# Transposes of the identity in TensorE's planned gaps, in the first ten pairs of an attention and gated-FFN kernel

## The chip, the cores and the metric

The kernel runs on one core of a Trainium2 chip. The metric is the device time of one execution in microseconds (us): the median of three runs before the change was 793.36 us (792.95 to 796.02).

## The reference

Inputs are q, k and v of shape 8 x 8 x 576 x 64 (batch, heads, sequence, head size), and the weights of a gated FFN. Cut to what matters:

```python
q_rot, k_rot = rotate(q), rotate(k)                      # rotary embedding
scores = (q_rot @ k_rot.T) / sqrt(64)
attn = exp(scores - max(scores)); attn /= sum(attn)      # over the last axis
x = (attn @ v), heads put side by side                   # 8 x 576 x 512
gate = sigmoid(sum over k of conv_w[k] * x shifted by 4 - k)   # 5 taps, causal
out = (gate * (x @ w_val)) @ w_out
```

Weights arrive as 64-bit floats and are decoded on the chip.

## The kernel before

**Work.** Two heads of one batch make a pair; there are 32 pairs, four to a batch. For one pair:

- q and k are loaded, rotated (`rope_mul`, `rope_add`) and split into a high and a low part (`qk_hi`, `qk_lo`).
- `s_mm` computes scores in five chunks, c = 0 to 4, of 128 query rows each: for c = 0 to 3 both heads, 12 matmuls, and for c = 4 the last 64 rows of both heads in 6. Each head's scores go into one PSUM tile `ps_s` of 128 x 2 x 512, two banks, of which columns 0 to 287 of each half are used. There are two such tiles at a time.
- `s_max` (VectorE, DVE) takes the negated row maximum `nm` from `ps_s`; `s_exp` (ScalarE, ACT) reads `ps_s` again and writes the exponentials `p`.
- `t_mm` transposes `p` on TensorE (PE), four blocks of 128 x 128 to a bank `ps_t`; `t_copy` copies them to `pt` in SBUF on ACT or DVE.
- `pv_mm` multiplies `pt` with v (`ps_a`), `x_norm` divides by the row sums, then come five taps (`tap`, most on DVE) and the gate.

After every fourth pair the FFN of that batch follows (`f_mm`, tiles `ps_f`). While the first pairs run, DVE, ACT and GpSimd (POOL) also decode the two weight matrices (`weight_step`, tile `wst`), in 12 pieces.

**Order.** All work is entered as jobs in a `Plan`, each with an engine, a duration in ns and what it reads and writes. `Plan.order` plays the jobs through in a timeline of its own, by these costs and a table of due times; it yields one order for all engines and leaves each job's start and end in `start` and `end`. `Plan.run` then calls the jobs' functions in that order. Each engine works through its instructions strictly in this order. Waits between engines are put in by the framework from the tiles' reads and writes: an instruction that writes a tile waits until those that came earlier in the order and read it have ended. In the plan a transpose costs 108.5 ns.

In the rows of order below, `ident` is the identity, `k_86` and `k_87` the rotated k of even and odd pairs, `q_88` and `q_89` the same for q. A wait on `Activation_49`, `DVE_49`, `Pool_49` or `PE_49` is one for ACT, DVE, POOL or PE itself to have got to a certain instruction. By the diff, line 291 before is line 311 after (`s_mm`), and 316 before is 336 after (`transpose`).

Of the kernel before, what the change touches and what calls it, by code (L numbers as in the profile page):

```python
# [10 lines left out]
F32 = mybir.dt.float32  # L11
# [43 lines left out]
class Plan:  # L55
# [11 lines left out]
    LAG = {"PE": 200, "V": 130, "A": 135, "G": 90, "SP": 100}  # L67
    WAIT = {"PE": 100, "V": 100, "A": 100, "G": 130, "SP": 40}
    SWITCH = 170

    def __init__(self):
        self.jobs = []
# [34 lines left out]
    def order(self, due=None):  # L107
# [40 lines left out]
        while len(done) < n:  # L148
# [11 lines left out]
            if m and m != mode:  # L160
                ns += self.SWITCH
                mode = m
# [17 lines left out]
        self.start, self.end = start, end  # L180
        return done

    def run(self):
        for i in self.order():
            self.jobs[i][3](*self.jobs[i][4])


@with_exitstack
def attn_gated_ffn(ctx: ExitStack, tc: tile.TileContext, q2, k2, v2, tab, w_val, conv_w, w_out, out, collect=None):
# [14 lines left out]
    V, A, G, T, SP = nc.vector, nc.scalar, nc.gpsimd, nc.tensor, nc.sync  # L204
# [9 lines left out]
    psS = ctx.enter_context(tc.tile_pool(name="psS", bufs=B["ps_s"], space=PSUM))  # L214
    psT = ctx.enter_context(tc.tile_pool(name="psT", bufs=B["ps_t"], space=PSUM))

    ident = const.tile([128, 128], F32, name="ident")
# [54 lines left out]
    def qk_lo(p, n, eng, a=0, b=W):  # L272
        t = state[p][n][:, :, a:b]
        eng.tensor_tensor(out=t[:, 1], in0=ins[n][:, 0, a:b], in1=t[:, 0].bitcast(F32), op=ALU.subtract)  # L274

    def s_mm(p, c):


        st = state[p]
        heads = (0,) if c == 4 else (0, 1)  # L280
        tiles = []
        for h in heads:
            ps = psS.tile([128, 2, 512], F32, name="ps_s", tag="ps_s")
            st[f"s{2 * c + h}"] = ps[:, :, 0:288]
            tiles.append(ps)
        for half in range(2):
            for i, (x, y) in enumerate(((0, 0), (0, 1), (1, 0))):
                for h in heads:
                    rows = slice(0, 128) if c == 4 else HEAD[h]
                    k0 = (0 if h else D) + half * 288  # L290
                    T.matmul(out=tiles[h][:, half, 0:288], lhsT=st["q"][rows, x, c * 128:c * 128 + 128],  # L291
                             rhs=st["k"][rows, y, k0:k0 + 288], start=(i == 0), stop=(i == 2))
# [260 lines left out]
    plan = Plan()  # L553
# [38 lines left out]
    for p in range(NP):  # L592
        t = 9 * p
# [31 lines left out]
        for c in range(5):  # L625
            r = kr + " " + toks(f"q{par}#@.@", ("hi", "lo"), (0,) if c < 2 else (1,))
            w = toks(f"ps_s/{p}.@", (2 * c, 2 * c + 1)) if c < 4 else f"ps_s/{p}.8"
            at(f"s{c}", t + 2 * c, "PE", 800, s_mm, p, c, r=r, w=w, mode="r" if c < 4 else "f")
            for i in (2 * c, 2 * c + 1)[:1 + (c < 4)]:
                h = i % 2  # L630
                at(f"max{i}", t + i, "V", 727, s_max, p, i, r=f"ps_s/{p}.{i}", w=f"nm/{p}.{i}")
                at(f"exp{i}", t + i, "A", 830, s_exp, p, i, r=f"ps_s/{p}.{i} nm/{p}.{i}",
                   w=f"p/{p}.{c}#{h} sums{par}#{i}" if i < 8 else f"p/{p}.m sums{par}#8")
# [23 lines left out]
        for g in R2:  # L657
            n = G1 if g else G0
# [58 lines left out]
    if collect is not None:  # L717
        return plan
    with tc.manual_schedule():
        plan.run()  # L720


# [36 lines left out]
def _program(arrays, batches):  # L759
    import concourse.bacc as _bacc  # L760

    nc = _bacc.Bacc("TRN2", target_bir_lowering=False, num_devices=1)
    args = [
        nc.dram_tensor(f"in_{n}", a.shape, mybir.dt.from_np(a.dtype), kind="ExternalInput").ap()
        for n, a in arrays.items()
    ]
    args.append(nc.dram_tensor("out_t", (batches, DM, S), F32, kind="ExternalOutput").ap())
    with tile.TileContext(nc, schedule_with_timeline_sim=True) as tc:
        attn_gated_ffn(tc, *args)
    return nc  # L770
# [9 lines left out]
```

## Time and profile before

| | |
|---|---|
| Median of three runs | 793.36 us |
| The profiled execution, and its span | 798.84 us, 797.0 us |
| PE busy | 730.3 us, 92% |
| PE weight loads (PEld) busy | 589.7 us, 74% |
| DVE busy | 604.5 us, 76% |
| ACT busy | 489.7 us, 61% |
| POOL busy | 414.5 us, 52% |
| Transposes of `p` (L316) | 1312, busy 202.2 us |
| Score matmuls (L291) | 1728, busy 184.4 us |
| Exponentials (L310) | 288, busy 212.0 us |
| Maxima (L297) | 288, busy 209.0 us |

The busy share is a mean over the span. PEclk is the TensorE clock that the throttle granted as a share of full speed; it is 1.00, 0.50 or, over a longer stretch, a mean of the two. In the profile's rows, what stands in brackets is the idle time of the engine ahead of the instruction, and what ended it.

### The profile page before, as it was taken

Reading aid. Unit: us, or ns where it says so; the run is one execution under the profiler, and the core shown is the slowest. Engines: PE = TensorE matmul, PEld = TensorE weight load, DVE = VectorE, ACT = ScalarE, POOL = GpSimd, SP = SyncE. Lnnn points to the kernel's source line nnn. Section 1 sums busy time; section 2 is a strip of 40 time slices with the busy share of each in tenths; the row PEclk is TensorE's granted clock in tenths of the full one; section 3 lists DMA queues with packets and bytes.
Section 4 is the critical chain, followed back from the end, with each engine's and each line's share of the span. In section 5 each row is a group of like instructions: output and inputs, shape, how many; then the busy total and the mean of one; then the engine's idle time right before and its main releaser. Section 6 shows DMA issues by size and latency. Waiting matters only on the chain.

```text
span 797.0 us, 16072 instructions
## 1 busy us (share of the span) xinstructions
PE 730.3 (92%) x5889; PEld 589.7 (74%) x5889; DVE 604.5 (76%) x994; ACT 489.7 (61%) x1155; POOL 414.5 (52%) x300
## 2 busy tenths in 40 slices
PE   1787678769999999999999999999999999999998
PEld 0655455557688878787878788788778887888798
DVE  4777998889987786778778777878677877776650
ACT  1546536654676666767667676766676676766542
POOL 2446454344745765566644665566755664551121
PEclk9989777899999999999999999999999999999999
DMA  7634323223333334433344223333443333410111
GB/s 186 154 83 109 92 74 105 74 57 105 87 93 100 85 77 114 114 104 91 104 109 112 71 71 110 103 90 92 113 115 93 92 101 105 111 37 24 37 47 60
DMA packets 92881, 73.76 MB, mean 93 GB/s; under 512 B 60633, under 2 KB 71426, under 8 KB 92802
## 3 DMA queue, kind: packets, MB, share of 16 engines
q1 hardware_dynamic: 91250, 71.51, 33.7%
q10 hardware_dynamic: 1552, 1.21, 0.6%
q8 instruction: 47, 0.77, 0.4%
q14 instruction: 32, 0.26, 0.1%
HBM read 63.10 MB, written 9.59 MB: 91 GB/s over the span
## 4 chain that ended last, share of the span: by engine, by line
PE 67%; DVE 10%; ACT 2%; issue 2%; DMA 1%; SPq 0%; POOLq 0%; POOL 0%; ACTq 0%; DVEq 0%
PE ps_f L458 22%; PE ps_a L371 16%; PE ps_t L316 15%; PE ps_s L291 15%; DVE nm L297 3%; DVE g L435 2%; ACT p L310 1%; DVE y L466 1%; DVE sums L382 1%; DVE wst L507 1%; DMA kin<-in_k 1%; ACT pt L357 1%; DVE pt L359 1%; PE ps_r L387 0%; DVE kin L263 0%
## 5 line engine op out<-in xcount | busy, mean ns | idle before, releaser
L310 ACT ACTIVATE p<-ps_s,nm 128x576 f32<-128x576 f32 x288 | 212.0, 740 | 120.9 <-DVE nm L297 119.2
L297 DVE TENSOR_REDUCE nm<-ps_s 128x1 f32<-128x576 f32 x288 | 209.0, 750 | 64.9 <-PE ps_s L291 63.0
L316 PE MATMUL ps_t<-ident,p 128*128 128x128 f32 x1312 | 202.2, 290 | 32.8 <-ACT p L310 27.6
L291 PE MATMUL ps_s<-k,q 64*128 64x288 f32 (+1 forms) x1728 | 184.4, 324 | 24.9 <-ACT k L270 16.5
L316 PEld LDWEIGHTS ps_t<-ident,p 128*128 128x128 f32 x1312 | 154.7, 147 | 70.8 <-ACT p L310 35.8
L291 PEld LDWEIGHTS ps_s<-k,q 64*128 64x128 f32 (+1 forms) x1728 | 144.7, 198 | 56.9 <-issue 20.0
L371 PE MATMUL ps_a<-pt,v 128*64 128x320 f32 (+1 forms) x1280 | 174.3, 418 | 0.0
L263 POOL TENSOR_TENSOR qin<-qin,tab_q 128x640 f32<-128x640 f32 x62 | 100.2, 1628 | 99.9 <-DMA qin<-in_q 99.9
L357 ACT COPY pt<-ps_t 128x512 f32<-128x512 f32 (+2 forms) x261 | 119.2, 467 | 35.6 <-PE ps_t L316 33.0
L371 PEld LDWEIGHTS ps_a<-pt,v 128*64 128x64 f32 x1280 | 87.4, 139 | 63.0 <-issue 13.6
L435 DVE SCALAR_TENSOR_TENSOR g<-x,cw,g 128x576 f32<-128x576 f32 (+2 forms) x132 | 117.1, 891 | 2.0 <-ACT g L432 1.8
L458 PE MATMUL ps_f<-y,wout_hi 128*128 128x288 f32 (+2 forms) x512 | 111.2, 304 | 2.4 <-ACT pt L357 2.3
L359 DVE COPY pt<-ps_t 128x512 f32<-128x512 f32 (+1 forms) x155 | 97.1, 629 | 14.3 <-PE ps_t L316 14.1
L274 POOL TENSOR_TENSOR q<-qin,q 128x640 fp32r<-128x640 f32 (+1 forms) x32 | 52.8, 1650 | 74.7 <-ACT q L270 67.9
L458 PEld LDWEIGHTS ps_f<-y,wout_hi 128*128 128x128 f32 x512 | 82.5, 188 | 5.0 <-ACT pt L357 3.5
L422 POOL TENSOR_TENSOR xl<-x,xh 128x576 fp32r<-128x576 f32 (+2 forms) x33 | 45.5, 1379 | 75.2 <-ACT xh L418 71.2
L473 POOL TENSOR_TENSOR y<-y,y 128x288 fp32r<-128x288 f32 (+2 forms) x64 | 55.6, 869 | 53.4 <-ACT y L470 53.3
L458 PE MATMUL ps_f<-xh,wval_hi 128*128 128x288 f32 (+2 forms) x256 | 77.6, 303 | 0.1
L458 PE MATMUL ps_f<-xl,wval_hi 128*128 128x288 f32 (+2 forms) x256 | 77.2, 301 | 0.0
L458 PE MATMUL ps_f<-y,wout_lo 128*128 128x288 f32 (+2 forms) x256 | 77.1, 301 | 0.0
L458 PE MATMUL ps_f<-xh,wval_lo 128*128 128x288 f32 (+2 forms) x256 | 76.0, 297 | 0.0
L267 POOL TENSOR_TENSOR kin<-kin 128x640 f32<-128x640 f32 (+1 forms) x32 | 49.1, 1533 | 34.5 <-DVE kin L263 33.6
(72 smaller groups left out, 784.7 us busy)
## 6 DMA issues: line engine op xcount, KB each, us to landing
kin<-in_k SPq DMA_DIRECT2D x62, 288.0 KB, 3.8
qin<-in_q SPq DMA_DIRECT2D x31, 512.0 KB, 4.2
out_t<-o SPq DMA_DIRECT2D x56, 144.0 KB, 2.9
rb<-rd SPq DMA_DIRECT2D x31, 144.0 KB, 3.0
v<-in_v SPq DMA_DIRECT2D x32, 128.0 KB, 2.3
v<-in_v SPq DMA_DIRECT2D x64, 64.0 KB, 2.3
rb<-rd SPq DMA_DIRECT2D x31, 128.0 KB, 2.9
qin<-in_q SPq DMA_DIRECT2D x64, 32.0 KB, 3.1
```

The costliest lines, as they stand in the source:

```text
L263: eng.tensor_tensor(out=t[:, i, a:b], in0=t[:, i, a:b], in1=tabs[n][:, i, a:b], op=ALU.mult)
L274: eng.tensor_tensor(out=t[:, 1], in0=ins[n][:, 0, a:b], in1=t[:, 0].bitcast(F32), op=ALU.subtract)
L291: T.matmul(out=tiles[h][:, half, 0:288], lhsT=st["q"][rows, x, c * 128:c * 128 + 128], rhs=st["k"][rows, y, k0:k0 + 288], start=(i == 0), ...
L297: V.tensor_reduce(out=st[f"nm{i}"], in_=st[f"s{i}"], axis=AX.XY, op=ALU.max, negate=True)
L310: A.activation(out=pd.rearrange("p (b x) -> p b x", b=2), in_=st[f"s{i}"], func=AF.Exp, bias=st[f"nm{i}"], scale=1.0, accum_out=sums[p % 2 ...
L316: T.transpose(out=bank[0:rows, j * 128:(j + 1) * 128], in_=src, identity=ident)
L357: A.copy(out=dst, in_=src)
L359: V.tensor_copy(out=dst, in_=src)
L371: T.matmul(out=acc[HEAD[h], 0:n], lhsT=st["v"][:, j, h, :], rhs=st[f"pt{g}"][:, at_:at_ + n], start=(j == 0), stop=(j == 4))
L435: V.scalar_tensor_tensor(out=g, in0=x_sb[:, a + k:b + k], scalar=w, in1=g, op0=ALU.mult, op1=ALU.add)
L458: T.matmul(out=acc[:, 0:n], lhsT=wt[w][:, kc, ds], rhs=mv, start=(kc == 0 and i == 0), stop=(kc == NCH - 1 and i == 2))
L473: G.tensor_tensor(out=ffn[b][1][:, dc, lo:hi], in0=ffn[b, "y", dc, lo], in1=ffn[b][0][:, dc, lo:hi].bitcast(F32), op=ALU.subtract)
```

## The change

`Plan.run` now looks, ahead of each PE job, at the plan's own timeline: t is the end of the PE job before (3000 ns at the start), and if the gap from t to the job's start, less 300 ns, holds more than two transposes of 110 ns, and t is under 230000 ns, that many transposes of the identity are issued ahead of the job. They write columns 384 to 511 of the newest `ps_s` tile, which no other instruction reads or writes. The first 80 come ahead of the first scores, and take the tile that these will use (`spare["next"]`).

```diff
+    FILL = (3000, 230000, 300, 110)
...
-    def run(self):
+    def run(self, fill):
+
+        t = self.FILL[0]
         for i in self.order():
+            if self.jobs[i][1] == "PE":
+                n = int((self.start[i] - t - self.FILL[2]) / self.FILL[3])
+                if n > 2 and t < self.FILL[1]:
+                    fill(n)
+                t = self.end[i]
             self.jobs[i][3](*self.jobs[i][4])
...
+    spare = {}
+
+    def fill(n):
+
+        if not spare:
+            spare["now"] = spare["next"] = psS.tile([128, 2, 512], F32, name="ps_s", tag="ps_s")
+        for _ in range(n):
+            T.transpose(out=spare["now"][:, 0, 384:512], in_=ident, identity=ident)
+
...
-            ps = psS.tile([128, 2, 512], F32, name="ps_s", tag="ps_s")
+            ps = spare.pop("next", None)
+            if ps is None:
+                ps = psS.tile([128, 2, 512], F32, name="ps_s", tag="ps_s")
+            spare["now"] = ps
...
-        plan.run()
+        plan.run(fill)
```

There are 374 such transposes: 80 at the start and 294 in 29 bursts of 3 to 21. Without them the order of every engine is the one before. One exponential gains a wait for PE.

PE's first instructions before, from the first scores of pair 0 on:

```order
L291 MATMUL ps_s<-k_86,q_88 128x288 [waits Activation_49]
L291 MATMUL ps_s<-k_86,q_88 128x288
L291 MATMUL ps_s<-k_86,q_88 128x288 [waits DVE_49]
L291 MATMUL ps_s<-k_86,q_88 128x288 x9
L316 MATMUL ps_t<-ident,p 128x128 [waits Activation_49,Pool_49]
L316 MATMUL ps_t<-ident,p 128x128 x3
L291 MATMUL ps_s<-k_86,q_88 128x288 [waits PE_49]
```

and the same place on PE after:

```order
L291 MATMUL ps_s<-ident 128x128 [waits Pool_49]
L291 MATMUL ps_s<-ident 128x128 x79
L311 MATMUL ps_s<-k_86,q_88 128x288 [waits Activation_49]
L311 MATMUL ps_s<-k_86,q_88 128x288
L311 MATMUL ps_s<-k_86,q_88 128x288 [waits DVE_49]
L311 MATMUL ps_s<-k_86,q_88 128x288 x9
L291 MATMUL ps_s<-ident 128x128 [waits Activation_49]
L291 MATMUL ps_s<-ident 128x128 x14
L336 MATMUL ps_t<-ident,p 128x128 x4
```

The first 80 wait only for POOL, which makes the identity. The burst of 15 stands between the scores and the transposes of `p`, and the wait for ACT stands at the burst; the transposes behind it have none of their own.

PE at the end of pair 0 and the start of pair 1 before (41.95 to 45.49 us in the profile):

```order
L316 MATMUL ps_t<-ident,p 128x128 [waits PE_49,Activation_49]
L316 MATMUL ps_t<-ident,p 128x128 [waits PE_49]
L316 MATMUL ps_t<-ident,p 128x128 x3
L291 MATMUL ps_s<-k_87,q_89 128x288
L291 MATMUL ps_s<-k_87,q_89 128x288 [waits PE_49]
L291 MATMUL ps_s<-k_87,q_89 128x288 [waits DVE_49]
L291 MATMUL ps_s<-k_87,q_89 128x288
L291 MATMUL ps_s<-k_87,q_89 128x288 [waits Pool_49]
L291 MATMUL ps_s<-k_87,q_89 128x288 x7
L316 MATMUL ps_t<-ident,p 128x128 [waits Activation_49]
L316 MATMUL ps_t<-ident,p 128x128 x3
```

and the same place on PE after:

```order
L291 MATMUL ps_s<-ident 128x128 [waits Activation_49]
L291 MATMUL ps_s<-ident 128x128 x13
L336 MATMUL ps_t<-ident,p 128x128 [waits PE_49] x2
L336 MATMUL ps_t<-ident,p 128x128 x3
L311 MATMUL ps_s<-k_87,q_89 128x288
L311 MATMUL ps_s<-k_87,q_89 128x288 [waits PE_49]
L311 MATMUL ps_s<-k_87,q_89 128x288 [waits DVE_49]
L311 MATMUL ps_s<-k_87,q_89 128x288
L311 MATMUL ps_s<-k_87,q_89 128x288 [waits Pool_49]
L311 MATMUL ps_s<-k_87,q_89 128x288 x7
L291 MATMUL ps_s<-ident 128x128 [waits Activation_49]
L291 MATMUL ps_s<-ident 128x128 x14
```

Bursts of 14 and 15 now stand ahead of the transposes on both sides of the scores of pair 1, and take over the wait for ACT.

## The prediction

> **What bounds the kernel now.** I read the slices of the page first, then the busy time by stage. Slices are 19.9 us wide.
>
> ```profile
> PE   1787678769999999999999999999999999999998
> DVE  4777998889987786778778777878677877776650
> PEclk9989777899999999999999999999999999999999
> ```
>
> ```profile
> 16.50:39.90 23.40, 17.98 (x87) 13.98 (x88) 18.38 (x32) 11.01 (x25) 10.74 (x9) 1.00 0.62 152
> 39.90:183.30 143.40, 106.81 (x727) 75.96 (x725) 123.05 (x197) 80.31 (x185) 66.41 (x43) 0.81 0.32 87
> 183.30:797.00 613.70, 605.54 (x5079) 499.75 (x5077) 456.62 (x741) 395.68 (x940) 333.22 (x239) 1.00 0.33 89
> ```
>
> Columns: width, then PE, PEld, DVE, ACT and POOL busy, granted clock, DMA. From 183.30 on PE is busy 605.54 of 613.70 us at full clock: it is the bound, and whatever PE is late by at 183.30 is late at the end. Before that PE is busy 106.81 of 143.40 us, DVE 123.05: neither is full. So only this part, where the clock is 0.81 on average, can gain, and a delay there goes to the end.
>
> Next the clock, in stretches of 3.41 us, the length of which all its recorded intervals are multiples. Columns: width, PE busy, clock.
>
> ```profile
> 39.89:43.30 3.41, 1.94 (x20) 1.00 0.23 40
> 43.30:46.71 3.41, 1.63 (x19) 1.00 0.40 136
> 46.71:50.13 3.42, 2.77 (x18) 0.50 0.01 1
> 50.13:53.54 3.41, 3.41 (x20) 0.50 0.29 89
> 60.37:63.78 3.41, 1.07 (x10) 1.00 0.52 127
> 63.78:67.19 3.41, 3.20 (x14) 0.50 0.50 156
> 67.19:70.61 3.42, 2.26 (x22) 1.00 0.00 1
> 84.26:87.67 3.41, 3.41 (x21) 0.50 0.38 141
> 176.42:179.83 3.41, 1.75 (x20) 1.00 0.00 0
> 179.83:183.25 3.42, 3.42 (x21) 0.50 0.60 174
> sum 34.13, PE 24.85; mean PE 2.48
> ```
>
> A stretch with 1.63, 1.07 or 1.75 us of PE work is followed by half clock, one with 1.94 is not: the fall comes somewhere between 1.75 and 1.94 of 3.41 us. From half clock it rises after a nearly full stretch (3.41, 3.20), not after 2.77. So PE work of any kind could hold the clock, if it lies in the idle time.
>
> What half clock costs a group, and where PE idles:
>
> ```profile
> 45.49 0.66 PE L316 MATMUL ps_t<-ident,p 128*128 128x128 f32 x4 [1.78 <-ACT p L310]
> 85.23 2.92 PE L316 MATMUL ps_t<-ident,p 128*128 128x128 f32 x14
> 262.52 0.87 PE ps_t L316 x8
> sum 54.60, PE 46.27; mean PE 5.14
> ```
>
> Transposes stream at 0.87/8 = 0.109 us each at full clock and 2.92/14 = 0.209 at half. The last row sums the nine half-clock stretches after 39.89: 46.27 us of PE work in 54.60. Before 39.89 the page writes 1.00 because no clock record exists yet; the rows below show the cold rate there (4 transposes in 1.08 us against 0.66).
>
> ```profile
> 16.53 0.61 PE L291 MATMUL ps_s<-k,q 64*128 64x288 f32 x2 [16.53 <-ACT k L270]
> 21.65 1.08 PE L316 MATMUL ps_t<-ident,p 128*128 128x128 f32 x4 [2.42 <-ACT p L310]
> PE ps_t L316 <- ACT p L310: 27.1, 16, 3.2
> PE ps_s L291 <- ACT p L310: 6.8, 7, 3.3
> DVE nm L297 <- PE ps_s L291: 13.8, 14, 3.8
> DVE pt L359 <- PE ps_t L316: 6.2, 10, 0.9
> L297 DVE TENSOR_REDUCE nm<-ps_s x56: 697/748/759, 19.9 to 178.9; 128x1 f32<-128x576 f32 x56
> ```
>
> The waits are those of 16.5 to 183.3 (us, times, longest). PE idles for an exponential (33.9 us), DVE idles for PE (20.0 us). It is one loop: scores, maximum, exponential, transposes and next scores.
>
> **The change part by part.** It adds 374 transposes in 30 bursts, and moves nothing else: each engine's own order is the same.
>
> *The first 80.* They wait only for the identity.
>
> ```profile
> 1.01 0.29 POOL masks.py:199 TENSOR_SCALAR_AFFINE_SELECT ident<-ident 128x128 f32<-128x128 f32 x1
> ```
>
> Ready at 1.30; 80 x 0.109 = 8.7 ends at 10.0, 80 x 0.209 = 16.7 ends at 18.0, against the first scores at 16.53. Ends: 0 and +1.5 us. I take 0, since a cold start of two stretches still ends near 13: 16 to 32 of them cold. The wait for DMA, ACT and DVE up to 16.53 covers them. Their warmth is gone by then, because 3 us of idle follow; I count no gain.
>
> *The other 294, in 29 bursts.* Where they stand decides. The plan sees PE idle because a transpose waits for an exponential. A burst writes columns 384 to 511 of the newest score bank, between the two halves that the exponential reads, and the order shows 21 of the 29 bursts beginning with a wait for ACT, three with one for DVE, five with none of their own. The values waited for are those of the exponential (or maximum) of that same bank. So a burst does not fill the idle time. It starts when the exponential has ended, which is when the real transposes would start, and they, the next scores and all behind them on PE stand in its queue. On the row at 45.49: 4 transposes started after the first exponential of the pair; now 15 dead ones start after the second.
>
> ```profile
> 45.34 0.73 ACT L310 ACTIVATE p<-ps_s,nm 128x576 f32<-128x576 f32 x1
> ```
>
> The second ends at 46.07, 0.6 later; 15 x 0.109 = 1.6; the four start at 47.7 instead of 45.49, 2.2 us late, without any idle time used.
>
> Cost in PE time: 294 x 0.109 = 32.0 us if all run warm, 294 x 0.209 = 61.4 if all cold. I take a third cold, because waits stay as long as they were and the long ones still make the clock fall: 196 x 0.109 + 98 x 0.209 = 41.9. The later start: 0.6 at some eight bursts, 5 us in all; ends 0 and 8.6, the upper with one burst that stands 3.6 us ahead of its exponential.
>
> Gain: half of the cold PE time, (17.98 + 46.27)/2 = 32.1 us, if no cold is left. With the same third left, 21.4; ends 8 (the clock falls as often, rises a stretch sooner) and 32.1.
>
> What of it reaches the end: DVE takes PE's lateness only where it waits for PE. There are 56 maxima in these stages, from 31 score products (5 for 9 maxima), and 14 had DVE waiting: 14/31 = 0.45 of it, for cost and gain alike. Elsewhere DVE's own work (taps, weight decoding, rotation) covers a late PE; without that cover the share would go to 1.
>
> Two rows show where it is uncovered and that gain and cost meet in the same place:
>
> ```profile
> 49.53 4.34 PE L371 MATMUL ps_a<-pt,v 128*64 128x256 f32 x20
> 55.49 1.42 DVE L297 TENSOR_REDUCE nm<-ps_s 128x1 f32<-128x576 f32 x2 [3.76 <-PE ps_s L291]
> ```
>
> The 20 products took 4.34 us at half clock; warm they would save 2, and the two bursts ahead of them (14 and 15) cost 3.2.
>
> Seven of the 294 lie past 183.3, on the full engine: within the 32.0.
>
> Sum: (41.9 + 5 - 21.4) x 0.45 = +11.5 us. The profiled execution took 798.84 (span 797.0), 5.5 above the median of the runs, 793.36; I put the sum on the median: 805. Bounds: (32.0 + 0 - 32.1) x 0.45 = 0, and (61.4 + 8.6 - 8) x 0.45 = +28, that is 793 and 821.
>
> Rule against row: in 84.26:87.67 at half clock, transposes are most of the work, and full clock follows.
>
> ```profile
> 84.26:87.67 3.41, 2.44 (x12) 2.44 (x13) 0.01 (x1) 0.41 (x1) 0.50 0.38 141
> ```
>
> That is the same stretch with the tile ps_t alone: 2.44 of 3.41 us. I take it that transposes count as activity. The Trainium skill, "TensorE: Matmul & The Clock Gate", section "Part 4: PE-mode transpose", says the opposite: in transpose mode the full clock does not engage, since it is not counted as PE-busy in the same way. By that rule the bursts would be pure cost, the third rival below. The trace so far speaks against it, though that stretch had 0.97 us of other matmuls.
>
> **The rivals.** *Faster:* the bursts hide, the clock does not. If DVE's own work covers the bursts (it is busy 86% of 39.90 to 183.30) while the cold products on the path, like the 20 above, run warm, the gain is 21.4 x 0.45 = 9.6 us: 784. It decides once less than 9.6 of the 46.9 us of cost, a fifth, reaches the path. For it: 17 of 31 products have no DVE waiting. Against: the same share covers the gain.
>
> *No change:* all warm, cost equal to gain, the lower bound above: 793. For it: 32.0 against 32.1. Against: a wait of 2.3 us or more stays idle in a stretch of 3.41.
>
> *Pure cost:* transposes do not hold the clock up: all at the cold rate where it was cold and no gain, (61.4 + 5) x 0.45 = 30: 823. Against: the row of 84.26.
>
> **How the numbers follow.** Likeliest (slower, 797.5 to 821): 0.54. Faster: 0.20. No change: 0.19. Pure cost: 0.07. A measurement of this kernel tells about 0.5%, 4 us, from nothing, so faster is below 789.4, slower above 797.3. Faster 0.20, same 0.19, slower 0.61. The range 786 to 822 leaves out half of the faster case and most of the last.
>
> **What would show it.** In the changed profile: transposes on the identity starting just after an exponential, PE idle ahead of them as long as ahead of the real ones before (waits for ACT p near 34 us up to 183 in all), and the real transposes directly behind; the clock less often at half, but still falling after waits over 2.3 us; the stretch in which PE becomes full begins some 10 us later than 183. Wrong would be: PE idle for exponentials fallen by 15 us or more, or a full clock from the first scores on with DVE's waits for PE well below 20 us (faster), or half clock as often as before (pure cost).

## The result, and the profile after

The changed kernel takes 818.18 us (median of four runs, 813.40 to 819.18) against 794.36 us before (four runs, 792.95 to 796.02): ratio 1.0287, 95% interval 1.0239 to 1.0335. It is 23.8 us slower; 11.5 were forecast. The profiled execution after took 817.29 us, span 815.5, which is 18.5 us above the profiled one of before; those two are compared below. The profiled execution of before, 798.84 us, lies above all four of those runs, so this pair shows some 5 us less than the medians; the run with the first 80 alone, below, gives a second measure.

The slices of the changed kernel (20.4 us wide), PE, DVE and granted clock:

```profile
PE   6788877878999999999999999999999999999998
DVE  5557868977988778777878786878768777777550
PEclk9889989998999999999999999999999999999999
```

From the fifth slice to the eighth the clock is higher than before (9, 8, 9, 9 against 7, 7, 7, 8 tenths), but it still falls, and PE becomes full a slice later. (The first two slices of before have no clock record and can't be compared.) To compare equal work, take the stretch from the first scores to the first FFN matmul. These are its busy rows (columns as in the prediction): first of the kernel before, then of the changed one, then the dead transposes alone in the same stretch of the changed one (PE and PEld only). The clock of the first row, 0.84, is too high: before 39.89 us nothing is recorded, and this counts as full. With those 23.4 us at half, as the cold rates there suggest, it would be 0.77 (an estimate).

```profile
16.53:189.25 172.72, 130.74 (x860) 93.30 (x860) 147.18 (x235) 93.57 (x215) 82.74 (x54) 0.84 0.36 96
```

```profile
15.31:207.43 192.12, 149.72 (x1147) 118.76 (x1147) 142.90 (x235) 92.70 (x215) 82.78 (x54) 0.89 0.33 88
15.31:207.43 192.12, 45.87 (x287) 38.68 (x287) 0.89 0.33 88
```

The stretch is 19.4 us longer (172.72 to 192.12). PE's idle time in it is unchanged: 172.72 - 130.74 = 41.98 before, 192.12 - 149.72 = 42.40 after. PE's busy time is 18.98 longer: the bursts put in 45.87, and the kernel's own matmuls need 130.74 - (149.72 - 45.87) = 26.9 less because less of them runs at half clock. (The last matmul of a burst and the first behind it overlap in the records, 55.55 against 55.35 us in the rows below. From all records of the trace, these overlaps come to 5.2 us: without the bursts, the kernel's own matmuls are busy 109.0 us, 21.7 less than before, and the bursts add 40.7. Either way the balance is 19.0.) So the bursts raised the clock, filled none of the idle time, and the difference went to the end whole. After the first FFN matmul nothing changed: 797.0 - 189.25 = 607.8 us before, 815.5 - 207.43 = 608.1 after.

How a burst sits, from the timeline of the changed kernel at the start of pair 1 (the second exponential of the pair on ACT, then PE):

```profile
52.06 0.73 ACT L330 ACTIVATE p<-ps_s,nm 128x576 f32<-128x576 f32 x1
52.93 2.62 PE L291 MATMUL ps_s<-ident 128*128 128x128 f32 x15 [2.50 <-ACT p L330]
55.35 1.06 PE L336 MATMUL ps_t<-ident,p 128*128 128x128 f32 x4
```

PE waits 2.50 us for the exponential, as it did before ahead of the real transposes (1.78 us at 45.49). Then 15 dead transposes run, partly at half clock, and only then the four real ones, which could have begun at the first exponential.

The waits in the same stretch, us in total, times and longest:

```profile
PE ps_s L291 <- ACT p L330: 33.7, 19, 3.9
DVE nm L317 <- PE ps_s L311: 31.0, 18, 4.7
DVE pt L379 <- PE ps_t L336: 14.5, 8, 4.3
```

The 33.7 us that PE waits for exponentials are the 33.9 of before; they now stand ahead of the bursts (L291). DVE's waits for PE have grown to 45.5 us; before, in the stretch from the first scores to the first FFN matmul, they were 14.1 + 6.2 = 20.3:

```profile
DVE nm L297 <- PE ps_s L291: 14.1, 15, 3.8
DVE pt L359 <- PE ps_t L316: 6.2, 10, 0.9
```

### The profile page after: what moved, and what is told of

The parts are those of the page before. It is cut to its first block, busy times and chain, and to the rows that moved or that the text cites. A ratio compares the mean times of both kernels' runs of the same rounds, so it can differ in the third digit from the quotient of the medians.

```text
span 815.5 us, 16811 instructions
## 1 busy us (share of the span) xinstructions
PE 760.8 (93%) x6263; PEld 626.6 (77%) x6263; DVE 603.1 (74%) x994; ACT 488.4 (60%) x1155; POOL 413.2 (51%) x300
## 4 chain that ended last, share of the span: by engine, by line
PE 70%; DVE 11%; ACT 3%; issue 3%; DMA 1%; SPq 0%; POOLq 0%; POOL 0%; ACTq 0%; DVEq 0%
PE ps_f L478 21%; PE ps_a L391 16%; PE ps_t L336 15%; PE ps_s L311 14%; DVE nm L317 3%; PE ps_s L291 3%; DVE g L455 2%; ACT p L330 2%; DVE y L486 1%; DVE sums L402 1%; DVE pt L379 1%; ACT pt L377 1%; DVE wst L516 1%; DMA kin<-in_k 1%; DVE wst L527 1%
## 5 line engine op out<-in xcount | busy, mean ns | idle before, releaser
L336 PE MATMUL ps_t<-ident,p 128*128 128x128 f32 x1312 | 194.3, 282 | 5.4 <-DVE x L430 4.3
L336 PEld LDWEIGHTS ps_t<-ident,p 128*128 128x128 f32 x1312 | 151.4, 144 | 36.7 <-issue 22.0
L311 PE MATMUL ps_s<-k,q 64*128 64x288 f32 (+1 forms) x1728 | 173.9, 313 | 3.3 <-ACT k L278 2.7
L391 PE MATMUL ps_a<-pt,v 128*64 128x320 f32 (+1 forms) x1280 | 170.4, 411 | 0.0
L311 PEld LDWEIGHTS ps_s<-k,q 64*128 64x128 f32 (+1 forms) x1728 | 137.0, 189 | 32.3 <-issue 20.0
L291 PE MATMUL ps_s<-ident 128*128 128x128 f32 x374 | 58.3, 318 | 39.6 <-ACT p L330 33.9
L291 PEld LDWEIGHTS ps_s<-ident 128*128 128x128 f32 x374 | 50.4, 164 | 45.6 <-ACT p L330 39.4
```

What stands on the lines that cost most here:

```text
L291: T.transpose(out=spare["now"][:, 0, 384:512], in_=ident, identity=ident)
L336: T.transpose(out=bank[0:rows, j * 128:(j + 1) * 128], in_=src, identity=ident)
L391: T.matmul(out=acc[HEAD[h], 0:n], lhsT=st["v"][:, j, h, :], rhs=st[f"pt{g}"][:, at_:at_ + n], start=(j == 0), stop=(j == 4))
```

## The experiments

Theory Q (queue): a burst starts when its exponential ends and holds PE's queue for its own length; all of this reaches the end, less the cold time recovered. Against it stood P (only the share 0.45 of the prediction arrives), S (the first 80 cost), L (the moved wait costs, not the length) and H (transposes slow other work or do not hold the clock). The runs of the kernel before on the same chip gave medians of 795.40 (first four experiments) and 795.13 us (the other four).

**Only the first 80** (`e1_first`)

```diff
-                if n > 2 and t < self.FILL[1]:
+                if n > 2 and t == self.FILL[0]:
```

> Only the 80 transposes ahead of the first scores are left; the 29 bursts are gone. Theory Q (queue): what costs is that each burst starts when its exponential ends and holds PE's queue for its own length, and this passes to the end in full, so the first 80 cost nothing: 792 to 797 us, the rest of the trace as before. Theory S (start): the 80 delay or chill the first scores and carry a good part of the 24 us: 800 us or more.

Measured: 796.47 us, ratio 1.0011 (0.9992 to 1.0031). S falls: no cost and no gain of the first 80 can be told from zero. The busy row from the first scores to the first FFN matmul:

```profile
14.28:183.96 169.68, 129.87 (x861) 91.17 (x861) 143.29 (x235) 93.34 (x215) 82.85 (x54) 0.79 0.37 100
```

PE idles 39.8 us here. The clock is recorded through the whole stretch and is 0.79 on average, near the 0.77 estimated for before. Against this execution (794.66 us) the stretch of the changed kernel is 192.12 - 169.68 = 22.4 us longer, 19.9 of it PE's busy time and 2.6 its idle time; the medians of the two kernels are 818.18 - 796.47 = 21.7 us apart.

**One transpose a burst** (`e7_one`)

```diff
-                    fill(n)
+                    fill(n if t == self.FILL[0] else 1)
```

> All 29 bursts are cut to one transpose each, at the same places with the same waits; the first 80 stay. Theory Q: 29 x 0.109 = 3 us of PE time, up to 5 us for transposes that now wait for the later of two exponentials, little clock gained: 796 to 802 us. Theory L (later start): the moved wait is what costs, so most of the 24 us stay: 806 us or more.

Measured: 801.20 us, ratio 1.0079 (1.0046 to 1.0113). The moved waits and 29 single transposes together cost 4.7 us over the run with the first 80 alone. In the profile PE is busy 129.58 of 175.83 us from the first scores to the first FFN matmul: its busy time is that of the run before, its idle time, 46.3 us, is 6.4 more. So the later start does cost some us, but L falls: most of the loss comes with the length of the bursts.

**Bursts of half the length** (`e4_half`)

```diff
-                    fill(n)
+                    fill(n if t == self.FILL[0] else n // 2)
```

> The bursts stand where the change put them, each at half its length (140 transposes in place of 294), the first 80 as they were. Theory Q: between one transpose a burst (801 us) and the full bursts (818 us), near the straight line: 801 + 17 x 113/267 = 808 us, 804 to 812. Theory K (the clock pays for short bursts): a shorter burst already keeps the clock up, so a dip below the line: 796 us or less.

Measured: 804.63 us, ratio 1.0139 (1.0096 to 1.0181). The straight line between one transpose a burst and the full bursts would give 808, and the measurement lies at the lower edge of the 804 to 812 around it. It is 3.4 us above single transposes, and the two intervals overlap a little. K falls: at half length the bursts do not pay for themselves at this place.

**Bursts of double length** (`e6_double`)

```diff
-                    fill(n)
+                    fill(n if t == self.FILL[0] else 2 * n)
```

> Each of the 29 bursts is twice as long (294 more transposes), the first 80 as they were. Theory Q: every transpose on the queue reaches the end: 294 x 0.109 to 0.13 = 32 to 38 us more, less some 5 us of half clock still to be recovered: 843 to 852 us. Theory P (the share of 0.45 that the prediction took): 818 + 0.45 x 30 = 831 us.

Measured: 849.68 us, ratio 1.0672 (1.0620 to 1.0725), 31.5 us above the changed kernel. That is 31.5/294 = 0.107 us for each of the added transposes, near the rate at which PE streams them (0.109): P falls. The busy row from the first scores to the first FFN matmul, the bursts alone, and the waits:

```profile
14.65:241.62 226.97, 182.74 (x1435) 151.79 (x1435) 142.75 (x236) 93.19 (x215) 79.88 (x54) 0.90 0.28 75
14.65:241.62 226.97, 82.58 (x574) 76.33 (x574) 0.90 0.28 75
DVE nm L317 <- PE ps_s L311: 51.3, 20, 6.2
DVE pt L379 <- PE ps_t L336: 25.4, 8, 4.6
```

The bursts put in 82.58 - 45.87 = 36.7 us more than in the changed kernel, the kernel's own matmuls take 103.85 - 100.16 = 3.7 less, so 33.0 us are added on PE; the stretch is 226.97 - 192.12 = 34.9 us longer. So the share that reaches the end is about 1 (that 0.107 equals the streaming rate so well is in part chance, since cold transposes and recovered clock offset each other in it). PE's idle time is 226.97 - 182.74 = 44.2 us, near that of the others. DVE does the same 143 us of work and waits 76.7 us for PE.

**Bursts into a bank that nobody reads** (`e5_free`). The burst now writes the `ps_t` bank which the job behind it allocates in any case. That bank was emptied by a copy some jobs earlier, so the burst no longer waits for an exponential. Seven bursts ahead of jobs that take no new `ps_t` bank are left out, 69 transposes.

```diff
-            T.transpose(out=spare["now"][:, 0, 384:512], in_=ident, identity=ident)
+            T.transpose(out=to, in_=ident, identity=ident)
...
+            spare["t"] = psT.tile([128, 512], F32, name="ps_t", tag="ps_t")
+            to = spare["t"][:, 384:512]
...
+    def bank(name):
+        return spare.pop("t", None) or psT.tile([128, 512], F32, name=name, tag="ps_t")
```

> The bursts write the ps_t bank that the PE job behind them takes anyway, instead of the score bank that the exponential reads; they then wait only for copies made long before. Seven bursts ahead of jobs that take no new ps_t bank are left out (69 of the 294 transposes). Theory Q: the bursts now run while PE waits, so they delay little and the clock stays up: PE idle between the first scores and the first FFN matmul falls from 42 us by about 20, time 780 to 796 us. Theory H (transposes of the identity slow the chip's other work, or hold no clock): 805 us or more.

Measured: 788.59 us, ratio 0.9916 (0.9893 to 0.9940): 0.8% faster than the kernel before, and 29.6 us under the median of the changed one. H falls: it is the same kind of work in another place. There are 225 transposes in place of 294, but the smaller number does not explain the gain, since 140 in the old place took 804.63 us. The busy row and the bursts alone up to the first FFN matmul, PE's waits (the third is that of the bursts) and DVE's for PE, then from the timeline the first exponential of pair 1 on ACT and PE around it:

```profile
15.13:175.36 160.23, 135.13 (x1079) 102.81 (x1079) 143.99 (x234) 93.01 (x215) 81.34 (x53) 0.94 0.40 106
15.13:175.36 160.23, 29.93 (x218) 26.68 (x218) 0.94 0.40 106
PE ps_t L347 <- ACT p L341: 11.2, 9, 2.3
PE ps_s L322 <- ACT p L341: 5.2, 10, 1.0
PE ps_t L299 <- ACT pt L388: 0.2, 1, 0.2
DVE nm L328 <- PE ps_s L322: 4.2, 5, 1.3
DVE pt L390 <- PE ps_t L347: 4.2, 6, 1.9
```

```profile
40.02 0.74 ACT L341 ACTIVATE p<-ps_s,nm 128x576 f32<-128x576 f32 x1 [1.86 <-DVE nm L328]
```

```profile
38.06 1.07 PE L322 MATMUL ps_s<-k,q 64*128 64x288 f32 x12
39.06 1.86 PE L299 MATMUL ps_t<-ident 128*128 128x128 f32 x15
40.91 0.66 PE L347 MATMUL ps_t<-ident,p 128*128 128x128 f32 x4
```

It is the same place as the one at 52.93 above: here the burst starts as soon as the scores are out and ends as the first exponential ends, and the real transposes follow with no wait. Idle falls from 41.98 to 160.23 - 135.13 = 25.1 us, the kernel's own matmuls from 130.74 to 105.2 (109.1 without the overlap), so of the 29.9 us of bursts about 16.9 lie in what was idle. DVE's waits for PE fall with it, to 4.2 + 4.2 = 8.4 us. In this pair of profiles the first FFN matmul is 13.9 us earlier than before (175.36 against 189.25), of which 1.4 come ahead of the first scores, and the span is 10.7 shorter (786.3); 3.2 us are given back behind the first FFN matmul, and why stays open. Between the medians the gain is 6.8 us.

**The same, at two thirds, at double length, and without the first 80**

```diff
 e8_free_short     fill(n if t == self.FILL[0] else 2 * n // 3, self.jobs[i])
 e10_free_double   fill(n if t == self.FILL[0] else 2 * n, self.jobs[i])
 e9_free_nofirst   if n > 2 and self.FILL[0] < t < self.FILL[1]:
```

> Bursts into the free bank at two thirds of their length (144 in place of 225), first 80 as they were. About 30 us of burst time filled only some 17 us of idle time in the full version, so the shorter ones should overrun less, but hold the clock up less well. If overrun is what still costs: 784 to 787 us. If the clock decides: 790 to 793 us.

Measured: 788.80 us, ratio 0.9925 (0.9900 to 0.9951), equal to the full bursts. It fits neither side of the expectation. In the profile, from the first scores to the first FFN matmul (17.09 to 178.36 us), the bursts take 22.64 us in place of 29.93, but PE idles 28.3 us in place of 25.1 and the kernel's own matmuls take 110.3 in place of 105.2: what is saved in dead work is lost again in clock and idle time.

> Bursts into the free bank at twice their length (450 in place of 225). Theory Q: what fits into idle time is free and the rest holds the queue in full; 25 us of PE idle were left ahead of the FFN, of which perhaps a third can be filled: 225 x 0.109 = 24.5 us, two thirds of it late, less up to 3 us of half clock: 800 to 806 us, well under the 31 us that doubling cost behind the exponentials.

Measured: 796.48 us, ratio 1.0010 (0.9983 to 1.0037). Below the 800 to 806 expected: the added 225 cost 7.9 us, 0.035 each, a third of what they cost behind the exponentials. So more of the idle time could be filled than I had allowed for, but twice the length brings the kernel back to where it was. The profile shows the filling, but not the median time, since it caught the fastest of the ten executions (789.65 us): from 15.84 to 179.46 us PE idles 11.8 us, and the bursts take 52.62.

> Bursts into the free bank without the 80 ahead of the first scores. If the 80 only warm a clock that falls again before the first scores: the same as with them, 786 to 791 us. If they matter once the bursts behind them hold the clock: 791 us or more.

Measured: 788.28 us, ratio 0.9905 (0.9873 to 0.9936): no use of the first 80 is seen here either.

## Why the prediction was wrong

The direction was right, and so was the place of the bursts in PE's queue; what the prediction had wrong is how much of PE's lateness reaches the end, and so the size was off by a factor of two. That 818 lies below the upper bound of 821 is luck: the bound was reached with bursts that all run cold and the share still at 0.45, and neither came true. By its steps:

- *Where the bursts stand.* Right. PE's waits for exponentials stayed (33.9 us, 33.7), the bursts start behind them, and moved to a bank that no exponential reads, 225 of the same transposes gain. The first FFN matmul came 18 us later (207.43 against 189.25), where some 10 were forecast.
- *The first 80.* Taken at 0, and 0 by the run that has only them.
- *Length of the bursts and later start.* For the length 41.9 us were forecast; the bursts, 287 of the 294, are busy 45.87, or 40.7 without the overlap. For the later start 5 us were forecast. PE's idle time grew by 0.4 us against the profile of before, by 2.6 against that of the first 80 alone, and by 6.4 with single transposes: some us, but the size is not settled.
- *Gain.* 21.4 us forecast; 26.9 measured, or 21.7 without the overlap. So the terms inside the bracket of the sum came out nearly as forecast. (Its row of 46.27 us at half clock covers nine intervals of one to four stretches, not nine stretches; the sum is right.) Waits stay long enough for the clock to fall, as forecast; two such places after, width, PE busy and clock:

```profile
128.95:132.37 3.42, 0.01 (x1) 1.00 0.36 80
132.37:135.78 3.41, 3.21 (x15) 0.50 0.02 3
163.09:166.50 3.41, 0.70 (x6) 1.00 0.00 0
166.50:169.91 3.41, 3.41 (x18) 0.50 0.88 211
```

- *The share that reaches the end.* This is the step that failed: 0.45 forecast, 1 measured. With its own costs and gain the sum at a share of 1 is 25.5 us; measured were 19.4 in the stretch against the profile of before, 22.4 against that of the first 80 alone, and 23.8 between the medians. Doubling the bursts measured the share by itself: 33.0 us more on PE made the stretch 34.9 longer. I had counted the score products for which DVE already waited (14 of 31), a share of occasions and not of time, and taken DVE's other work as cover for the rest. But a later PE made DVE wait where it had not: its waits for PE went from 20.3 to 45.5 us and, with double bursts, to 76.7, by 25 and 31 us for stretches 19 and 35 us longer; with bursts in the free bank they fell to 8.4. DVE's work at 86% was no cover: the prediction itself says that scores, maximum, exponential and transposes are one loop, and DVE stands in it. PE's idle time, 42.0 before, 42.4 after and 44.2 us with double bursts, says the same from the other side: nothing of the lateness was made up. That the fixed order of each engine is the reason why DVE could not use the time is argued, not shown; no run changed the order.
- *The rivals.* Pure cost (transposes do not hold the clock) is refuted by the start of the changed kernel, where PE runs nothing but transposes:

```profile
1.36 11.23 PE L291 MATMUL ps_s<-ident 128*128 128x128 f32 x80 [1.36 <-POOL ident masks.py:199]
```

```profile
2.66:6.07 3.41, 3.41 (x18) 3.41 (x17) 1.00 0.92 247
6.07:9.49 3.42, 3.42 (x34) 3.42 (x33) 1.00 1.04 239
```

18 of them go by in one stretch and 34 in the next (no clock is recorded before 6.07 us, so the 1.00 of the first row is no reading): they start at the cold rate, 3.41/18 = 0.19 us each, and raise it themselves to 3.42/34 = 0.10. It does not rise unasked: before, PE does nothing until 16.53 us and still runs cold behind that (four transposes in 1.08 us at 21.65). The Trainium skill, "TensorE: Matmul & The Clock Gate", section "Part 4: PE-mode transpose", has it that transposes do not engage the full clock; in this kernel, with 32-bit transposes, they do. The faster rival had it that DVE's work covers the bursts; no such cover is seen, and a gain, 6.8 us, came only with bursts that lie in PE's own idle time. No change wanted cost and gain equal with everything warm; the clock still fell, and the bursts cost nearly twice what they gained.

## What to carry to other kernels

Filler work helped here only where its operands were free when the gap opened: if it writes or reads what the engine is waiting for, it starts when the gap ends and lengthens the queue by all its time. Before counting on cover from a second engine, ask whether that engine stands in the same loop of waits; here it did, and lateness passed in full although DVE was busy 86% of the time. Idle time of the engine between two fixed points of the program, before and after, shows at once whether filler went into the gaps.

## What the runs showed of the hardware

Transposes alone brought the clock from half to full (18 in the stretch before 6.07 us, 34 in the one after). The prediction put the fall of the clock somewhere between 1.75 and 1.94 us of PE work in a stretch. The edge is less sharp than that:

```profile
111.89:115.30 3.41, 1.76 (x18) 1.00 0.54 165
115.30:118.71 3.41, 3.27 (x16) 0.50 0.00 0
```

After 1.76 us of work in a stretch it fell; but after the 1.64 us of the one below it stayed full, so what counts is not just the busy time of one stretch as the profile has it.

```profile
135.78:139.19 3.41, 1.64 (x14) 1.00 0.27 76
139.19:142.61 3.42, 3.42 (x33) 1.00 0.00 0
```
